# Splitting the column DFT of an FNet and gated-MLP kernel by the parity of its rows

## Chip, cores and metric

The kernel runs on one core of a Trainium2 chip, in one launch. The metric is device time in microseconds (us), the median of several runs. The engines are named as in the profile: PE is TensorE's matmul, PEld its weight load, DVE is VectorE, ACT is ScalarE, POOL is GpSimd, SP is SyncE, whose queue issues most of the DMA transfers.

## The reference

Four residual sublayers act on x of 2048 rows and 640 columns; the same two alternate twice.

```python
def mix(x):      # sublayer A: real part of a 2D DFT
    a = x @ hid_re.T ; b = x @ hid_im.T          # DFT over the 640 columns
    return seq_re @ a - seq_im @ b               # DFT over the 2048 rows, real part
def glu(x):      # sublayer B
    return (sigmoid(x @ w_gate) * (x @ w_up)) @ w_down     # 640 -> 1728 -> 640
x = x + mix(layernorm(x)); x = x + glu(layernorm(x))
x = x + mix(layernorm(x)); x = x + glu(layernorm(x))
```

The layernorms have no weights; eps is 1e-5. Everything is float32.

## The kernel before

x stays in SBUF as 16 tiles of 128 rows (`X`), in four row sets i of four groups A, B, C, D. A group holds rows that the symmetries of the row DFT pair with the others' rows, so one row set needs 128 rows of the DFT matrix. Each float32 operand of a matmul is split into two float16 parts, HI and LO, and each product is three matmuls (HI HI, HI LO, LO HI; `PASSES`). ACT makes the HI part and DVE the LO part (lines 241 and 243).

**A layer's mixing** has these steps. *Folding* normalizes a row set and adds or subtracts mirrored columns (`fold_columns`: e holds c and 640 - c added, o subtracted, 320 columns each; column 0 is doubled and appended to e) and mirrored rows (`fold_rows`, `fold_join`), and splits the result. *Sequence* (line 846) is the row DFT: for a row set i and a half tp (EV or OD, the even and odd output rows) it adds into three PSUM banks, one for each block d of 128 folded columns; row sets 0 and 1 make the sums ph = 0, row sets 2 and 3 ph = 1. *Eviction* (`evict_sums`) splits the sums into tiles z. *Hidden* (q, ph) is the column DFT (`product`, line 923): for r = 0 (real) and r = 1 (imaginary) it multiplies 128 rows of z with the folded column matrix, 321 output columns, over three blocks d of the contraction; 17 matmuls in all, since the last block of r = 1 has 64 rows and holds two parts in one tile. q 0 and 1 need the EV half, q 2 and 3 the OD half. `hidden_middle` does one row more. The products of ph = 0 and 1 are evicted separately; `combine` makes the difference and the sum of r = 0 and 1, `join_hidden` the sum or difference over ph, and `add_hidden` adds the 321 columns and their mirror images to x.

**The gated MLP** works in four blocks b of 512 rows. Block 0 begins with ordinary products (`gate_up`, line 1134); the first three tiles j are done in halves of 256 rows, since rows 0 and 1 are ready first. Later ones multiply 2 x 2 blocks in seven products instead of eight (line 1181). Then come the down products (line 1338), which add to x.

**The order** of the opening (loading and mixing of layer 0, to the first gate halves) is written out by hand as one list, `OPENING`: all instructions of all engines are issued in that order, and each engine works its own in order. In it `turn` are PE's row reversals, `col`, `double`, `re`, `ro`, `de`, `do`, `join`, `jhi`, `jlo` fold, `seq` is a sequence, `evhi` and `ev` evict sums, `hid` is a hidden product, `nst`, `npow`, `nscale`, `nrm`, `nhi`, `nlo` normalize, `tp` transposes, `gu` is a gate half, `wld`, `wshi`, `wslo` load and split a weight. After it `steps` lists PE's work in order, and `at(u, f)` puts another engine's job in front of step u. The layer change is the stretch between the last down product of layer 0 and the first gate half of layer 1; there `he` counts the steps.

**Space** in SBUF is one tile, `big`, in units of 128 float32 columns. Some places are fixed; the others come from `Slots`, which hands out space while the program is built: of the first few places that fit, it takes the one that was freed longest ago.

At the end the kernel tests that the given DFT matrices have the symmetries that it uses, and otherwise runs a general version.

Of the kernel before, what the change touches and what calls it, by code (L numbers as in the profile page):

```python
# [30 lines left out]
EC = EH + 1  # L31
EPS = 1e-5
# [39 lines left out]
FIX = XU + 2 * XTU + WDU  # L72


class Slots:

    LOOK = {4: 2, 5: 6}

    def __init__(self, big):
        self.big = big
        self.live = {}
        self.freed = {}
        self.clock = 0
        self.close = False

    def take(self, n, high):
        taken = sorted(self.live.values())
        if self.close:  # L90

            ends = [FIX] + [d for _, d in taken]
            free = [(a, b) for a, b in zip(ends, [c for c, _ in taken] + [UNITS]) if a + n <= b]
            assert free, f"no room for {n}: {taken}"
            if high:
                a = [a for a in range(UNITS - n, FIX - 1, -n) if all(a + n <= c or d <= a for c, d in taken)][:high]
                if a:
                    return self.new(min(a, key=lambda a: max(self.freed.get(u, 0) for u in range(a, a + n))), n)
                a = max(b for _, b in free) - n
            else:  # L100
                a = min((a for f in free for a in {f[0], f[1] - n}),
                        key=lambda a: (max(self.freed.get(u, 0) for u in range(a, a + n)), a))
            return self.new(a, n)
        found = []
        for i in range(UNITS):
            a = UNITS - (i + 1) * n if high else FIX + i * n
            if a < FIX or a + n > UNITS:
                break
            if all(a + n <= c or d <= a for c, d in taken):
                found.append(a)  # L110
                if len(found) == self.LOOK.get(n, 3):
                    break
        if not found:
            found = [a for a in range(FIX, UNITS - n + 1) if all(a + n <= c or d <= a for c, d in taken)][:1]
        assert found, f"no room for {n}: {taken}"
        age = lambda a: max(self.freed.get(u, 0) for u in range(a, a + n))
        return self.new(min(found, key=age), n)

    def new(self, a, n):
        s = Slot(self.big[:, a * UNIT : (a + n) * UNIT], (a, a + n))  # L120
        self.live[id(s)] = s.span
        return s

    def give(self, s):
        self.clock += 1
        del self.live[id(s)]
        for u in range(*s.span):
            self.freed[u] = self.clock


class Slot:
    def __init__(self, ap, span):
        self.f32, self.span = ap, span
        self.f16 = ap.bitcast(F16)
        n = self.f16.shape[1] // 2
        self.parts = (self.f16[:, :n], self.f16[:, n:])
# [16 lines left out]
    turn 0 B, turned 0 B, turn 0 C, turned 0 C, turn 1 B, chi 0 0, means 0, chi 1 0, square 0 C, stats 0 A,  # L153
    col 0 0, stats 0 D, turned 1 B, turn 1 C, col 0 1, clo 0 0, square 0 B, turned 1 C, clo 1 0, double 0 0,
    smeans 0, double 0 1, stats 1 A, means 1, stats 1 D, col 1 0, col 1 1, chi 1 1, square 1 B, clo 1 1,
    square 1 C, power 0, turn 2 B, double 1 1, turned 2 B, turn 2 C, scale 0, stats 2 A, ro 0 0, chi 1 2, chi 0 1,
    smeans 1, turned 2 C, whhi 1, col 2 0, double 1 0, power 1, re 0 0, clo 1 2, ro 0 1, scale 1, whhi 2, ro 1 1,
    col 2 1, re 1 0, re 1 1, ro 1 0, do 1 1, re 0 1, do 0 0, de 1 0, means 2, de 1 1, stats 2 D, square 2 B,
    do 1 0, de 0 1, de 0 0, join 1 o, square 2 C, whhi 5, do 0 1, join 0 e, row 0, join 0 o, smeans 2, whhi 0,
    join 1 e, whlo 1, whlo 0, row 1, double 2 0, power 2, jhi 0 e, jhi 0 o, turn 3 B, turned 3 B, c512hi, jhi 1 e,  # L160
    clo 0 1, turn 3 C, double 2 1, jhi 1 o, jlo 0 o, jlo 0 e, scale 2, col 3 0, row 2, jlo 1 o, turned 3 C, ro 2 1,
    re 2 1, jlo 1 e, col 3 1, chi 0 2, ro 2 0, re 2 0, whlo 5, de 2 1, do 2 0, double 3 0, seq 0 1, means 3,
    stats 3 A, do 2 1, double 3 1, seq 1 1, de 2 0, square 3 B, evhi 0 1 0, seq 0 0, join 2 o, join 2 e,
    square 3 C, wshi 0 1, stats 3 D, clo 0 2, row 3, whhi 3, whlo 2, ev 0 1 0, smeans 3, evhi 0 1 1, evhi 0 1 2,
    c512lo, ev 0 1 1, chi 1 3, whhi 4, jhi 2 o, whlo 3, whlo 4, ev 0 1 2, jhi 2 e, power 3, seq 1 0, wshi 2 0,
    scale 3, wshi 2 1, re 3 1, jlo 2 o, jlo 2 e, ro 3 1, chi 0 3, de 3 1, hid 3 0, evhi 0 0 0, evhi 0 0 2, do 3 1,
    re 3 0, clo 0 3, seq 2 1, ro 3 0, hidev 3 0, ev 0 0 0, clo 1 3, do 3 0, ev 0 0 2, join 3 o, de 3 0, evhi 0 0 1,
    jhi 3 o, ev 0 0 1, join 3 e, jhi 3 e, jlo 3 o, seq 2 0, wshi 1 0, jlo 3 e, hid 0 0, wslo 1 0, seq 3 0, difhi 0,
    wshi 1 1, evhi 1 0 0, evhi 1 0 1, wslo 1 1, dif 0, seq 3 1, evhi 1 0 2, ev 1 0 0, ev 1 0 1, ev 1 0 2,
    evhi 1 1 2, wslo 0 1, ev 1 1 2, evhi 1 1 0, evhi 1 1 1, hid 0 1, hid 1 0, ev 1 1 0, wld 3 1, difhi 1, ev 1 1 1,  # L170
    dif 1, sum 0, hid 2 0, wshi 0 0, add 0, hidev 1 0, hid 1 1, nst 0, sum 1, nst 1, npow 0, hidev 2 0, hidev 1 1,
    hid 3 1, add 1, nscale 0, hid 2 1, nrm 0, nst 3, nhi 0, nrm 1, wld 4 0, nhi 1, nst 2, nlo 0, nlo 1, tp 0,
    wslo 0 0, npow 1, wld 4 1, hidev 3 1, wshi 4 0, tpl 0, tp 1, midhi, tpl 1, nscale 1, tph 0, tph 1, wshi 4 1,
    hidev 2 1, nrm 2, mid, nhi 2, nrm 3, nhi 3, gu 0 0, middif, nlo 2, tp 2, wld 3 0, wslo 2 0, tpl 2, nlo 3,
    gu 1 0, tp 3, wshi 3 1, wshi 3 0, wslo 2 1, tph 2, tph 3, gu 2 0, wslo 3 1, tpl 3, gu 0 1, gu 1 1, gu 2 1,
    wslo 3 0, wslo 4 0, wslo 4 1"""

ON_ACT = {(2, GA), (2, GD), (3, GA), (3, GD)}
NORM_ACT, APPLY_ACT, COPY_ACT = {0, 3}, {3}, {3}
# [3 lines left out]
def kernel(ctx: ExitStack, tc: tile.TileContext, x, ct, wh, wg, wu, wc, wd, out):  # L183
# [7 lines left out]
    flag = pool.tile([P, 1], I32, name="flag")  # L191
    with tc.manual_schedule():
        folded(ctx, tc, pool, dram, big, acc, flag, x, ct, wh, wg, wu, wc, wd, out)
# [7 lines left out]
def folded(ctx, tc, pool, dram, big, acc, flag, x, ct, wh, wg, wu, wc, wd, out):  # L201
    nc = tc.nc
    slots = Slots(big)
# [3 lines left out]
    hs = pool.tile([P, 1], F32, name="hs")  # L207
# [77 lines left out]
    def drop(*key):  # L285
        s = held.pop(key if len(key) > 1 else key[0])
        if s.span:
            slots.give(s)
# [9 lines left out]
    def free_bank(*ks):  # L298
        banks.extend(ks)
# [297 lines left out]

    def folds(i):
        if (FE, i) not in held:
            if folding[0] and i < NB - 1:  # L600

                at = XU + i % 2 * XTU
                fixed(at, 11, FE, i)
# [1312 lines left out]
```

## Time and profile before

| what | value |
|---|---|
| time before, median of 3 runs | 1143.38 us (1143.14 to 1143.42) |
| span of the profiled execution | 1142.6 us, 23152 instructions |
| time outside the profiled span | the runs are 0.5 to 0.8 us over the span; the page gives no other time of that execution |
| mean granted clock of TensorE | 0.997 |
| matmuls of the column DFT (L923), 321 columns | 224 of 128 rows, 48 of 65 rows, 12 and 6 for the middle |
| matmuls of the row DFT (L846) | 288 |
| matmuls of the gates and down products (L1181, L1338, L1134) | 4698, 2624, 705 |
| DMA | 215.94 MB, 189 GB/s |

The profile gives busy time by engine, 40 slices of the span, and for groups of instructions the line, the operation, its shape, count, busy time and mean duration. [...] In an answer of the timeline a row is a run of like instructions on one engine: start, length, engine, line, operation, tiles, shape, count, and in brackets the idle time before it and what ended that. In the list of waits a row is: who waited, for whom, the total in us, how often, the longest.

### The profile page before, as it was taken

The numbers are of one execution on the slowest core, as the hardware profiler recorded it, in microseconds if no ns is written. First come the engines' busy times: TensorE is split into PE (matmuls) and PEld (weight loads), VectorE is DVE, ScalarE is ACT, GpSimd is POOL, SyncE is SP. The second block draws the span as 40 slices with busy tenths as digits, with TensorE's granted clock in tenths as the row PEclk, the third lists the DMA queues.
The fourth block names the chain that finished last, engine by engine and source line by source line (L and its number), as shares of the span: only waits on it lengthen the run. The fifth ranks groups of instructions, "written<-read, shape, count | busy, mean of one in ns | idle before, by whom it ended". The sixth has DMA issues, their size and how long they took to land.

```text
span 1142.6 us, 23152 instructions
## 1 busy us (share of the span) xinstructions
PE 1107.9 (97%) x8918; PEld 876.1 (77%) x8918; DVE 757.1 (66%) x1686; ACT 521.8 (46%) x1129; POOL 372.3 (33%) x584
## 2 busy tenths in 40 slices
PE   5599999999999999999999999999999999999997
PEld 2377446788878887888877888778887888788875
DVE  7995888867756777576657767815773568526740
ACT  5975475254524653265524445314551455225420
POOL 2313574432545454422430136021453113221000
PEclk9999999999999999999999999999999999999999
DMA  8427587858495868867412377575658853896401
GB/s 256 145 67 258 199 310 210 256 189 265 153 261 179 263 205 163 276 227 263 155 70 93 106 224 213 133 240 182 210 150 234 285 179 124 159 250 205 149 18 38
DMA packets 156434, 215.94 MB, mean 189 GB/s; under 512 B 74720, under 2 KB 101493, under 8 KB 156314
## 3 DMA queue, kind: packets, MB, share of 16 engines
q1 hardware_dynamic: 137754, 166.44, 48.1%
q0 software_dynamic: 18560, 47.93, 13.8%
q8 instruction: 72, 1.18, 0.4%
q14 instruction: 48, 0.39, 0.1%
HBM read 173.45 MB, written 26.26 MB: 175 GB/s over the span
## 4 chain that ended last, share of the span: by engine, by line
PE 89%; DVE 5%; DMA 2%; ACT 2%; issue 1%; POOL 1%; SPq 0%; DVEq 0%; POOLq 0%; ACTq 0%
PE acc L1181 42%; PE acc L1338 31%; PE acc L1134 10%; PE acc L1274 2%; PE acc L923 2%; PE acc L846 1%; DMA big<-in_ct 1%; DVE big L243 1%; PE twin L355 1%; DMA big<-kept_w 0%; DMA big<-in_wd 0%; DVE big L715 0%; DVE big L673 0%; DVE big L1009 0%; DVE big L707 0%
## 5 line engine op out<-in xcount | busy, mean ns | idle before, releaser
L1181 PE MATMUL acc<-big 128*128 128x256 f16 x4698 | 516.4, 273 | 0.2 <-ACT big L1185 0.2
L1181 PEld LDWEIGHTS <-big 128*128 128x128 f16 x4698 | 459.7, 98 | 54.6 <-issue 0.3
L1338 PE MATMUL acc<-big 128*128 128x320 f16 x2624 | 357.7, 299 | 0.0
L1338 PEld LDWEIGHTS <-big 128*128 128x128 f16 x2624 | 256.8, 98 | 99.5
L1387 POOL DMA_DIRECT2D big<-in_ct x256 | 174.8, 688 | 217.0 <-DVE big L1396 132.8
L1185 ACT ACTIVATE big<-acc 128x256 f32<-128x256 f32 x348 | 128.6, 380 | 237.0 <-PE acc L1181 235.6
L1371 ACT ACTIVATE big<-big 128x768 f32<-128x768 f32 (+8 forms) x104 | 79.6, 765 | 118.4 <-DVE big L1396 83.4
L1249 DVE TENSOR_TENSOR big<-big 128x512 f16<-128x512 f32 x87 | 59.9, 688 | 100.3 <-ACT big L1248 100.0
L1134 PE MATMUL acc<-big 128*128 128x256 f16 (+1 forms) x705 | 114.8, 325 | 1.1 <-DVE big L243 1.1
L1134 PEld LDWEIGHTS <-big 128*128 128x128 f16 x705 | 68.6, 98 | 46.2 <-DVE big L243 1.6
L1353 DVE SCALAR_TENSOR_TENSOR big<-acc,big 128x320 f32<-128x320 f32 x64 | 28.4, 484 | 99.4 <-PE acc L1338 99.3
L1227 ACT ACTIVATE big<-big 128x512 f32<-128x512 f32 x87 | 53.5, 627 | 45.2 <-DVE big L1218 44.6
L243 DVE SCALAR_TENSOR_TENSOR big<-big 128x640 f16<-128x640 f32 (+5 forms) x80 | 64.3, 839 | 9.9 <-ACT big L241 6.8
L241 ACT ACTIVATE big<-big 128x640 f16<-128x640 f32 (+6 forms) x80 | 50.2, 667 | 36.3 <-DMA big<-big 11.0
L1237 DVE SCALAR_TENSOR_TENSOR big<-acc,big 128x256 f32<-128x256 f32 x87 | 36.3, 418 | 40.5 <-PE acc L1181 34.4
L1404 POOL DMA_DIRECT2D big<-in_ct x40 | 27.3, 685 | 109.7 <-ACT big L1185 65.3
L1218 DVE TENSOR_TENSOR big<-big,acc 128x512 f32<-128x512 f32 x87 | 59.1, 679 | 3.6 <-PE acc L1181 3.4
L1248 ACT ACTIVATE big<-big 128x512 f16<-128x512 f32 x87 | 54.5, 626 | 9.6 <-DVE big L1239 8.8
L1217 DVE TENSOR_TENSOR big<-big 128x256 f32<-128x256 f32 x87 | 36.3, 417 | 15.6 <-ACT big L1185 15.5
L521 ACT ACTIVATE big<-big 128x384 f16<-128x384 f32 (+2 forms) x48 | 28.8, 648 | 29.3 <-DVE big L503 15.7
L1394 DVE TENSOR_TENSOR big<-big 128x256 f32<-128x256 f32 x64 | 26.8, 419 | 21.3 <-DMA big<-in_ct 21.2
L923 PE MATMUL acc<-big 128*128 128x321 f16 (+2 forms) x290 | 40.9, 300 | 0.0
(206 smaller groups left out, 1040.9 us busy)
## 6 DMA issues: line engine op xcount, KB each, us to landing
big<-kept_s SPq DMA_DIRECT2D x84, 512.0 KB
big<-kept_w SPq DMA_DIRECT2D x115, 320.0 KB
big<-in_ct POOLq DMA_DIRECT2D x256, 128.0 KB, 4.1
big<-kept_w SPq DMA_DIRECT2D x74, 192.0 KB
kept_w<-big SPq DMA_DIRECT2D x27, 320.0 KB
big<-in_ct POOLq DMA_DIRECT2D x32, 256.0 KB, 5.0
kept_s<-big SPq DMA_DIRECT2D x13, 512.0 KB
big<-in_wg SPq DMA_DIRECT2D x18, 320.0 KB
```

The lines of the kernel that those rows point to most:

```text
L243: nc.vector.scalar_tensor_tensor(dl, src, s, dh, op0=OP.mult, op1=OP.subtract)
L923: nc.tensor.matmul(ps[:m, :EC], z[:, at : at + m], w[:, 384 * wp : 384 * wp + EC], start=(d == 0 and zp == HI and wp == HI), stop=(d == ND ...
L1134: nc.tensor.matmul(ps, w[wp][:, d * P : (d + 1) * P], xt[:, xp, :], start=(d == 0 and wp == HI and xp == HI), stop=(d == ND - 1 and wp == LO))
L1181: nc.tensor.matmul(ps, wt, xt, start=start and n == 0, stop=n == len(todo) - 1, skip_group_check=not start)
L1185: nc.scalar.activation(dst, ps, AF.Copy)
L1218: nc.vector.tensor_tensor(v, v, other, op=OP.add)
L1227: nc.scalar.activation(v, v, AF.Sigmoid, scale=SG)
L1248: nc.scalar.activation(s.parts[HI], v, AF.Copy)
L1249: nc.vector.tensor_tensor(s.parts[LO], v, s.parts[HI], op=OP.subtract)
L1338: nc.tensor.matmul(held["pd", e][0][:, :EH], held["ht", j].parts[hp][:, i * P : (i + 1) * P], held["w", 2, j].parts[wp][:, e * EH : (e + 1 ...
L1371: nc.scalar.activation(v, v, AF.Square, accum_out=new_sum()[:p])
L1387: nc.gpsimd.dma_start(v[:, g], bass.AP(ct.tensor, (r * S + row) * S, [[P, NS], [d * S, 16], [1, P]]))
```

## The change

1. The 320 or 321 rows of the folded column matrix are sorted by parity. Output column 320 - k of an even row equals column k, and of an odd row it is column k negated. So even rows and odd rows are multiplied apart, for columns 0 to 160 only (161 columns, `EW`). Block d = 0 holds even rows, block 2 odd rows (161 columns each), block 1 both (322 columns, `EQ`; the rows of the wrong parity have scale 0). `unfold` makes the 321 columns by an addition and a subtraction. `fold_columns` writes the folded columns sorted by parity, reading every second column.
2. In the opening for all q, and in layer 1 for q = 0, the products of ph = 0 and 1 add into the same PSUM banks. After ph = 0 ACT copies the partial product; after ph = 1 the total is evicted, and the difference over ph comes as twice the part less the total.
3. The layer change begins with hidden (1, 0) and the odd half of row sets 0 and 1, which before stood ahead of the last down products; row set 3 is folded and joined for the even half first, and the last down product of layer 0 is done in two halves of columns. Hidden (0, 0) and (0, 1) follow, then the odd half; rows 0 and 1 are normalized first, rows 2 and 3 later. Hidden (3, 1) stands behind the first gate half.
4. `OPENING` has a new order. PE's order at its end, before and after:

```text
before: seq 0 1, 1 1, 0 0, 1 0, hid 3 0, seq 2 1, 2 0, hid 0 0, seq 3 0, 3 1, hid 0 1, 1 0, 2 0, 1 1, 3 1, 2 1,
        tp 0, tp 1, mid, gu 0 0, tp 2, gu 1 0, tp 3, gu 2 0, gu 0 1, gu 1 1, gu 2 1
after:  seq 0 1, 0 0, 1 1, 1 0, 2 1, 2 0, 3 0, 3 1, hid 0 0, 0 1, 1 0, 2 0, 1 1, 2 1,
        tp 0, tp 1, mid, gu 0 0, tp 2, gu 1 0, tp 3, hid 3 0, 3 1, gu 2 0, gu 0 1, gu 1 1, gu 2 1
```

5. The space of all tiles is planned ahead: the program is built once to record when each tile is taken and given back (counted in such events), `find_homes` gives each a place, and the program is built again with these places. In the first blocks of layer 1, the jobs that add row sets 2 and 3 to x come earlier.
6. The test at the end also covers the new symmetry (three more tests for each of r = 0 and 1).

The diff, cut to its core:

```diff
+EW = EH // 2 + 1
+EQ = 2 * EW
+NEAR = (60, 25, 8, 1)
...
+def find_homes(asked):
+    area = [n * (t1 - t0) for n, t0, t1 in asked]
+    for near in NEAR:
+        first = {}
+        for turn in range(40):
+            order = sorted(range(len(asked)), key=lambda k: (-first.get(k, 0), -area[k]))
+            homes, k = place_in_order(asked, order, near)
+            if k is None:
+                return homes
+            first[k] = first.get(k, 0) + 1
+def place_in_order(asked, order, near):
...
+            gap = min([t0 - u1 if u1 <= t0 else u0 - t1 for c, d, u0, u1 in placed if c < a + n and a < d] or [near])
+            rank = (min(gap, near), -a)
+            if best is None or rank > best[0]:
+                best = rank, a
...
     def product(ps, ph, r, at, m, more=False):
-        for d, n in enumerate(KT[r]):
+        for d, c in ((1, slice(0, EQ)), (0, slice(0, EW)), (2, slice(EW, EQ))):
+            n = KT[r][d]
...
-                    nc.tensor.matmul(ps[:m, :EC], z[:, at : at + m], w[:, 384 * wp : 384 * wp + EC],
+                    nc.tensor.matmul(ps[:m, c], z[:, at : at + m], w[:, 384 * wp : 384 * wp + c.stop - c.start],
...
     def hidden(q, ph):
         def mm():
-            pair = held["py", q, ph] = bank_pair()
-            for r in range(2):
-                product(pair[r][0], ph, r, sums_at(q, ph, r), P)
+            more = joined(q) and ph == 1
+            if not more:
+                held["py", q, ph] = bank_pair()
+            pair = held["py", q, 0 if more else ph]
+            for r in (1, 0) if q == 0 else (0, 1):
+                product(pair[r][0], ph, r, sums_at(q, ph, r), P, more)
...
+    def unfold(s, v, on=nc.vector):
+        on.tensor_tensor(s[:, :, :EW], v[:, :, :EW], v[:, :, EW:], op=OP.add)
+        on.tensor_tensor(s[:, ::-1, EH : EW - 1 : -1], v[:, :, : EW - 1], v[:, :, EW : EQ - 1], op=OP.subtract)
...
+    def first_sums():
+        (a, ka), (_, kb) = held.pop(("py", 0, 0))
+        o, t = pair_of(take(6, "sum", 0)), held["im"].f32[:, :EQ]
+        for n, op in enumerate((OP.subtract, OP.add)):
+            nc.vector.scalar_tensor_tensor(o[:, n], a[:, :EQ], CY, t, op0=OP.mult, op1=op)
...
     def join_hidden(q, cd):
         u, v = (pair_of(held["dif", q, ph]) for ph in range(2))
-        o = pair_of(take(6, "sum", q, cd))
-        nc.vector.tensor_tensor(o, u, v, op=OP.subtract if cd else OP.add)
+        if cd == 0 and q not in joins:
+            nc.vector.tensor_tensor(v, u, v, op=OP.add)
         if cd:
+            nc.vector.scalar_tensor_tensor(v, u, 2.0, v, op0=OP.mult, op1=OP.subtract)
...
+        unfold(whole_of(take(6, "out", q, cd)), v)
...
-            order = [(hidden, 0, 0), (hidden, 1, 0), (sequence, 2, EV), (sequence, 2, OD), (sequence, 3, EV),
-                     (sequence, 3, OD), (hidden, 0, 1), (hidden, 2, 0), (hidden, 3, 0), (hidden, 1, 1), (hidden, 2, 1),
-                     (hidden, 3, 1), (hidden_middle,)]
+            order = [(hidden, 1, 0), (sequence, 0, OD), (sequence, 1, OD), (sequence, 2, EV), (sequence, 3, EV),
+                     (hidden, 0, 0), (hidden, 0, 1), (sequence, 2, OD), (sequence, 3, OD), (hidden, 1, 1), (hidden, 2, 0),
+                     (hidden, 3, 0), (hidden_middle,), (hidden, 2, 1)]
             steps += [f(*a) for f, *a in order]
-            steps += [gate_up(0, j, (0,)) for j in range(3)]
+            steps += [gate_up(0, 0, (0,)), hidden(3, 1)] + [gate_up(0, j, (0,)) for j in (1, 2)]
...
-                steps += [sequence(*s) for s in early_sums]
+                steps += [sequence(i, EV) for i in range(2)]
...
-                at(block[0] + 1.6 + 0.8 * n if q == 1 else (block[0] + 14.6 if q == 2 else block[1] + 3.5) + n, f, q, *a)
+                at(block[0] + 1.6 + 0.8 * n if q == 1 else block[0] + (9.6 if q == 2 else 15.6) + n, f, q, *a)
```

422 lines of the change are left out of this document (256 added, 166 removed).

## Prediction

> **What bounds the kernel now.** I read the page's busy times and its slices first, then what TensorE (PE) waited for, then busy time by stretch, and last the timeline of PE.
>
> ```profile
> PE 1107.9 (97%) x8918; PEld 876.1 (77%) x8918; DVE 757.1 (66%) x1686; ACT 521.8 (46%) x1129; POOL 372.3 (33%) x584
> PE   5599999999999999999999999999999999999997
> ...
> PE acc L1181 <- ACT big L1185: 0.2, 1, 0.2
> ```
>
> PE is busy for 1107.9 us of a span of 1142.6. In the slices its idle time lies in the first two and the last; between them it waited 0.2 us for all the seven-product steps (L1181). So PE time saved in the middle would be time saved, unless something else comes due late. The change touches two places only: the opening and the layer change.
>
> ```profile
> 60.00:70.00 10.00, 9.50 (x84) 7.68 (x82) 9.97 (x19) 6.35 (x12) 0.00 (x0) 1.00 0.17 55
> 70.00:80.00 10.00, 10.00 (x76) 7.21 (x74) 9.68 (x17) 6.31 (x15) 1.24 (x2) 1.00 0.29 98
> ```
>
> The columns are stretch, length, busy time (and count) of PE, PEld, DVE, ACT and POOL, clock, DMA share and rate. From 60 to 70 us VectorE (DVE) is full and PE is not: the opening's front is DVE's. From 70 to 80 both are full, and neither can grow unseen.
>
> **The column products.** Seventeen matmuls of 321 columns become six of 322 and eleven of 161, in each of 16 products. The two middle products go from nine of 321 to three of 322 and six of 161.
>
> ```profile
> 603.73 4.82 PE L923 MATMUL acc<-big 128*128 128x321 f16 x34
> 608.38 4.89 PE L846 MATMUL acc<-big 128*128 128x256 f16 x41
> 613.56 3.56 PE L846 MATMUL acc<-big 128*128 128x256 f16 x31 [0.29 <-DVE big L715]
> 616.96 14.13 PE L923 MATMUL acc<-big 128*128 128x321 f16 x102
> ...
> 632.83 1.39 PE L923 MATMUL acc<-big 128*1 128x321 f16 x9
> 634.16 6.72 PE L1134 MATMUL acc<-big 128*128 128x256 f16 x60
> 640.72 1.40 PE L569 MATMUL acc<-ident,big 128*128 128x128 f16 x20
> ...
> L923 PE MATMUL acc<-big 128*128 128x321 f16 x224 | 34.1, 300 | 0.0
> ...
> L569 PE MATMUL acc<-ident,big 128*128 128x128 f16 x80 | 6.0, 220 | 0.4 <-DVE big L465 0.4
> ```
>
> A run's length less one matmul's own duration, over the others, is the spacing. 321 columns: (4.82 - 0.30)/33 = 137 ns. 128: (1.40 - 0.22)/19 = 62 ns. 256, from 60 in 6.72 us: 110 ns. No row has 161 columns; the line from 128 to 321 gives 62 + 33 x 0.39 = 75 ns, and half of 137 is 69. I take 72. A product goes from 17 x 137 = 2.33 us to 6 x 137 + 11 x 72 = 1.61, so 0.72 saved; a middle from 1.23 to 0.84. In all 16 x 0.72 + 2 x 0.39 = 12.3 us of PE, where PE sets the time.
>
> [...]
>
> **The layer change.** VectorE takes up the last down product at 603.79 (L1353, below) and the first gate half starts at 634.16: 30.4 us. In it PE did eight products (4.82 + 14.13 us), 72 sequence matmuls, 20 transposes, the middle, and waited some tenths (0.29 at 613.56). After the change, 36 matmuls of early sums come into this stretch, and it starts 36 x 0.11 = 4.0 us sooner. PE's work is 8 x 1.61 + 108 x 0.11 + 1.3 + 0.84 = 26.9 us. Without waits the gate half comes 30.4 - (26.9 - 4.0) = 7.5 us sooner. Two chains could take that back.
>
> The first runs from the last down product to row set 3's even half. It took 9.8 us (603.79 to 613.56).
>
> ```profile
> 603.79 0.89 DVE L1353 SCALAR_TENSOR_TENSOR big<-acc,big 128x320 f32<-128x320 f32 x2 [9.21 <-PE acc L1338]
> 604.60 0.87 DVE L420 BATCH_NORM_STATS2 quad<-big 128x6 f32<-128x320 f32 x2
> 605.51 0.21 DVE L421 BATCH_NORM_AGGREGATE quad<-quad 128x2 f32<-128x12 f32 x1
> ...
> 605.83 0.82 DVE L627 TENSOR_TENSOR big<-big 128x640 f32<-128x640 f32 x1
> ...
> 608.43 0.88 DVE L964 SCALAR_TENSOR_TENSOR big<-acc,big 128x321 f32<-128x321 f32 x2
> 610.18 1.69 DVE L707 TENSOR_TENSOR big<-big 128x321 f32<-128x321 f32 x4
> 611.88 1.62 DVE L715 TENSOR_TENSOR big<-big 128x642 f16<-128x642 f32 x2
> ```
>
> Half of the residual, of the statistics and of the two column folds now comes before the end, and half of the joins and splits after the even half: 0.44 + 0.44 + 0.82 + 0.84 + 0.81, and the 0.88 of L964 is gone. That leaves 5.6 us; with ACT's copies between, up to 7. The cover is one product and three sequences, 1.6 + 54 x 0.11 = 7.5 us, so it costs nothing; if the chain came out as before, it would cost 2.3.
>
> The second runs from the end of product 0 over both halves to the transposes of rows 0 and 1.
>
> ```profile
> 619.48 0.44 ACT L959 ACTIVATE big<-acc 128x321 f32<-128x321 f32 x1 [1.73 <-PE acc L923]
> ...
> 621.74 1.56 DVE L1009 TENSOR_TENSOR big<-big 128x642 f32<-128x642 f32 x2
> ...
> 623.34 0.74 ACT L430 ACTIVATE big<-big 128x640 f32<-128x640 f32 x1 [3.42 <-DVE big L1009]
> ...
> 624.20 0.83 ACT L431 ACTIVATE big<-big,small 128x640 f32<-128x640 f32 x1
> ...
> 625.74 0.72 POOL L404 TENSOR_TENSOR small<-small,half 128x2 f32<-128x2 f32 x1 [0.29 <-DVE small L403]
> 626.49 0.16 DVE L408 TENSOR_TENSOR small<-small 128x2 f32<-128x2 f32 x1 [0.84 <-POOL small L404]
> ...
> 63.42 0.68 DVE L243 SCALAR_TENSOR_TENSOR big<-acc,big 128x512 f16<-128x512 f32 x1
> ```
>
> Step by step: copy 0.44, sum and difference 0.89, two unfolds 0.88 (two halves of L707's kind), addition 1.56, row 1's statistics on ACT 1.8 (both passes with their read-outs), two small steps and the power 1.1, four small steps 0.8 (0.2 apart), one scaled copy 0.74, two low parts 1.6: 9.8 us. Three evictions of the odd half (0.68 each) stand in DVE's queue between: 11.4 with part of them hidden. PE's cover is two sequences and three products, 3.9 + 4.8 = 8.7, and 0.6 of transposes that run inside the wait. I take a wait of 2.0; it lies between none and 4. The gain here is 7.5 - 2.0 = 5.5 us, from 3.5 to 7.5.
>
> The new wait, product 0's second half behind ACT's copy of the first, is short: the products run r = 1 first, so a 0.44 copy has the 0.85 us of r = 0's nine matmuls to finish in. Queued behind it on PE are the sequences of the odd half, whose operands are ready by then. For rows 2 and 3 the same steps follow, with a doubling in place of the sums, again some 9.8 us; the cover is the middle, two products and two half-gates of 30 matmuls, 0.8 + 3.2 + 6.6 = 10.6. I book nothing, and 0.5 if it is short.
>
> **The opening.**
>
> ```profile
> 15.17 0.21 POOL L377 TENSOR_SCALAR quad<-quad 128x2 f32<-128x2 f32 x1 [3.38 <-ACT big L369]
> ...
> 34.48 2.88 POOL L377 TENSOR_SCALAR quad<-quad 128x4 f32<-128x4 f32 x1 [6.70 <-ACT big L369]
> ...
> 40.42 0.17 DVE L408 TENSOR_TENSOR quad<-quad 128x4 f32<-128x4 f32 x1 [0.18 <-POOL quad L404]
> ...
> 70.42 14.13 PE L923 MATMUL acc<-big 128*128 128x321 f16 x102
> ...
> 73.42 0.89 DVE L964 SCALAR_TENSOR_TENSOR big<-acc,big 128x321 f32<-128x321 f32 x2 [0.19 <-ACT big L959]
> ...
> 83.90 1.50 DVE L465 TENSOR_TENSOR big<-big 128x640 f16<-128x640 f32 x2
> ...
> 109.68 15.50 PE L1134 MATMUL acc<-big 128*128 128x512 f16 x71 [1.14 <-DVE big L243]
> ```
>
> Up to the last join the new list gives DVE the same work, less one eviction of 0.68. So the front ends 0.7 us sooner. The other end: a split (0.68) and two low parts (1.62 and a copy, 0.2) that stood before row set 2's scale (40.42, released by POOL) now stand after it; if POOL is no sooner, DVE is idle there for 2.5 us. I take the first: L377 took 0.21 us at 15.17 and 2.88 here, so POOL has that much to give back.
>
> The two products that PE did in the front's idle time (3 0, 0 0) now come later. After the sequences at 70.4 both products 0 follow, to 73.6, and the copy, 74.0. Then DVE: sums 0.89, unfolds 0.88, add 1.56, differences 0.88 and their doubling 0.8, statistics 1.09 (L420's two and L421), unfolds 0.88, add 1.56, an eviction 0.68, small steps 0.8, statistics 1.09, two low parts 1.64: 12.8, to 86.8, where L465 ended at 85.4. That is 1.4 later, 0.7 with the shorter front. PE's own four products end at 80, so it waits here for DVE, as it didn't before; product 2 1 also stands behind the eviction that DVE does after the second add. After the transposes PE has the middle's 0.4 us less and two products (3 0, 3 1) more, 3.2; the wait of 1.14 at 109.68 goes, since PE gets there later than its weights. Opening: 0.7 - 0.4 + 3.2 - 1.1 = 2.4 us lost, between -3.0 and +6.
>
> **What is hidden.** Folding and unfolding by two:
>
> ```profile
> 37.72 0.68 DVE L243 SCALAR_TENSOR_TENSOR big<-big 128x516 f16<-128x516 f32 x1
> ...
> 660.00:700.00 40.00, 40.00 (x361) 35.18 (x360) 25.94 (x63) 19.25 (x48) 15.69 (x23) 1.00 0.86 246
> ...
> SPq L1100 <- PE acc L1181: 111.8, 26, 15.0
> ...
> 262.50 5.51 DMA big<-kept_w
> ```
>
> L243's 516 elements are read every second one, and take the 0.68 us of the 512 read in a row: the strided folds cost nothing. In the second layer the unfolds add 1.76 us of DVE for each of three row sets (two of 0.88), 5.3 in all, in first blocks where DVE has 14 us idle in 40; at full DVE they would cost their 5.3. In the first layer it is half of that, as an addition goes for most of it. Six more checks of the column matrix stand beside the seven-product steps (the 0.2 us). The column matrix's loads carry half the bytes. In SP's queue two weight loads (3 1, 4 1) come to stand behind others that wait for splits of about the same time; if they came late, the 1.14 us at 109.68 would stay.
>
> Sum: 1143.4 - 5.5 + 2.4 = 1140.3 us, 3.1 less. The profiled span is 0.8 under the median of the runs; I carry the difference to the median. A measurement can tell 0.2%, 2.3 us: under 1141.1 is faster, over 1145.7 slower.
>
> **The rivals.** (1) Both chains fit under PE: 7.5 less at the layer change, and in the opening PE sets all after 70.4 (8 x 1.61 + 0.84 against 14.13 + 1.39, and no wait): 1.8 + 1.1 less. 1133.0. For: in the old chain DVE stood idle for POOL (0.84 at 626.49), and steps could fill that. Against: DVE's 9.68 of 10 us from 70 on.
>
> (2) Weight loads set the narrow matmuls:
>
> ```profile
> L923 PEld LDWEIGHTS <-big 128*128 128x128 f16 x224 | 21.9, 98 | 8.8 <-DVE big L243 0.2
> ```
>
> At 98 ns instead of 72, a product loses 0.29; eight at the layer change and four in the opening: 3.4 us, 1143.7, no change. For: 98 is what a load shows. Against: transposes at 62 ns with the same load.
>
> (3) The opening's front gets DVE's gap of 2.5 us and doesn't end 0.7 sooner: 3.2 more, 1143.5, no change. For: the scale waited for POOL before as well (0.18). Against: POOL's 0.21.
>
> (4) Slower: the planned homes. A load waits until the space that it gets is free, and all loads behind it on SP wait too. They wait now (111.8 us at L1100, 15.0 once), but PE feels 0.2. The chain passes through a load at 262.50 with no slack; a home freed only when the last reader before it is done would put its 5.51 us flight before PE, twice (weights and their sums) 11.0: 1151.3. It decides from 5.4 us on, one flight. For: the plan ranks by events, not by time. Against: it asks for up to 60 events between uses.
>
> **How the numbers follow.** Forecast 0.50, itself 1137.5 to 1142.5 (0.42 of it faster); (1) 0.11, (2) 0.08, (3) 0.12 (0.02 of it slower, where its tail adds), (4) 0.19. Faster 0.53, same 0.26, slower 0.21. The range leaves out (4) and the end of (1): 1134.0 to 1147.0.
>
> **What would show it.** Runs of product matmuls of 161 columns with about 72 ns spacing; PE busy for 12 us less; the first gate half 5 to 6 us nearer to the last down product's end, counted with the moved sums; PE idle before the transposes near 80 to 85 us; 512-column gates starting 2 us later than 109.68. It is wrong if PE waits for loads in the blocks, if the narrow matmuls space at 98, or if the opening's gates start earlier.

## The result: 1156.66 us, slower by 1.2%, and the profile after

| | before | after |
|---|---|---|
| median | 1143.39 us (1143.14 to 1143.42, 4 runs) | 1156.66 us (1155.6 to 1158.21, 4 runs) |
| profiled execution: span, own time | 1142.6 us, none shown | 1154.3 us, 1156.14 us |
| PE busy | 1107.9 us | 1101.6 us |

The ratio is 1.0116, interval 1.0101 to 1.013. The forecast was 1140.3 us, 1134.0 to 1147.0: wrong in sign. One remark on the sums: in later runs of the kernel before, 1.8 us lay between span and time (1142.0 and 1143.77, for one), so the profiled execution of before, at 1142.6, was probably some 1.0 us slower than the median, and a sum over the two profiles comes out nearer to 12 us than to the 13.3 of the medians.

First the page of the kernel after: busy time by engine, and PE's slices. The same rows of before stand in the prediction.

```profile
PE 1101.6 (95%) x8918; PEld 872.5 (76%) x8918; DVE 772.3 (67%) x1738; ACT 531.4 (46%) x1156; POOL 365.9 (32%) x573
PE   5479999999999999999999999999999999999997
```

PE is busy for 6.3 us less, and the span is 11.7 us longer: PE waits where it didn't. The list of its waits (total, how often, longest) has these among others; the first row is of before, at the same reversals of row sets. From 70 us on, before had one wait of 1.14 us at the first 512-column gates and some tenths elsewhere:

```profile
PE twin L355 <- ACT big L361: 12.0, 6, 7.5
```

```profile
PE twin L382 <- ACT big L388: 15.6, 6, 10.7
...
PE acc L1313 <- ACT big L1317: 4.2, 5, 1.2
...
PE acc L1266 <- ACT big L265: 2.9, 2, 2.5
...
PE acc L1003 <- DVE big L267: 2.1, 1, 2.1
PE acc L1003 <- ACT big L1054: 1.7, 1, 1.7
PE acc L1470 <- ACT big L1456: 1.6, 1, 1.6
```

L382 and L1003 are the opening, L1266 and L1470 layer 0's block 0, L1313 the seven-products, nearly all of it (3.6) in layer 1. Dividing the span at three places of PE's timeline gives a ledger in us (A: start to the first 512-column gate product; B: from there to the end of layer 0's down products; C: the layer change, to layer 1's first seven-product; D: the rest). In before, B holds 36 matmuls of early sums (4.0 us) that after has in C. The other columns are experiments told below; the last row has the medians. A to D are of one profiled execution each: the columns "mixed homes" and "+ three edits" have the same opening, and their A differs by 1.4 us.

| | before | after | mixed homes | + three edits | + front's order | + row set 3's product |
|---|---|---|---|---|---|---|
| A | 107.9 | 114.8 | 114.0 | 115.4 | 110.7 | 108.8 |
| B | 495.9 | 498.8 | 490.9 | 490.4 | 491.3 | 490.4 |
| C | 57.6 | 55.3 | 55.3 | 55.3 | 55.3 | 55.3 |
| D | 481.0 | 485.4 | 484.6 | 482.0 | 481.6 | 481.7 |
| median | 1143.4 | 1156.7 | 1147.4 | 1143.9 | 1140.1 | 1138.0 |

With the 4.0 us counted on the same side, after against before is +6.8 in A, +6.9 in B, -6.3 in C and +4.4 in D.

**C did what it should.** PE's timeline of after at the layer change:

```profile
613.38 1.76 PE L1003 MATMUL acc<-big 128*128 128x322 f16 x17
614.97 8.04 PE L921 MATMUL acc<-big 128*128 128x256 f16 x72
622.85 3.45 PE L1003 MATMUL acc<-big 128*128 128x322 f16 x34
...
634.84 0.44 PE L632 MATMUL acc<-ident,big 128*128 128x128 f16 x5
635.89 1.25 PE L632 MATMUL acc<-ident,big 128*128 128x128 f16 x15 [0.60 <-DVE big L510]
...
639.60 2.57 PE L1266 MATMUL acc<-big 128*128 128x256 f16 x22
```

A product takes 614.97 - 613.38 = 1.59 us, where 1.61 was forecast; neither chain keeps PE waiting for more than 0.6 us. The first gate half starts 26.1 us behind the last down product, where before took 30.3; with the 4.0 us of sums counted it is 8.2 us nearer, and 1.6 of these are product (3, 1), which now stands behind it.

### The profile page after: what moved, and what is told of

Same layout as the page of the kernel before. It is cut to its first block, busy times and chain, and to the rows that moved or that the text cites. A ratio compares the mean times of both kernels' runs of the same rounds, so it can differ in the third digit from the quotient of the medians.

```text
span 1154.3 us, 23256 instructions
## 1 busy us (share of the span) xinstructions
PE 1101.6 (95%) x8918; PEld 872.5 (76%) x8918; DVE 772.3 (67%) x1738; ACT 531.4 (46%) x1156; POOL 365.9 (32%) x573
## 5 line engine op out<-in xcount | busy, mean ns | idle before, releaser
L1313 PE MATMUL acc<-big 128*128 128x256 f16 x4698 | 516.8, 273 | 4.2 <-ACT big L1317 4.2
L1313 PEld LDWEIGHTS <-big 128*128 128x128 f16 x4698 | 459.6, 98 | 59.2 <-issue 5.1
L1470 PE MATMUL acc<-big 128*128 128x320 f16 x2624 | 357.9, 299 | 1.6 <-ACT big L1456 1.6
L1470 PEld LDWEIGHTS <-big 128*128 128x128 f16 x2624 | 256.7, 98 | 101.3 <-ACT big L1456 1.9
L1503 ACT ACTIVATE big<-big 128x768 f32<-128x768 f32 (+10 forms) x110 | 81.6, 742 | 120.3 <-DVE big L1528 86.8
L1266 PE MATMUL acc<-big 128*128 128x256 f16 (+1 forms) x705 | 117.0, 327 | 3.8 <-ACT big L265 2.9
L1266 PEld LDWEIGHTS <-big 128*128 128x128 f16 x705 | 68.5, 98 | 50.6 <-ACT big L265 3.9
L267 DVE SCALAR_TENSOR_TENSOR big<-big 128x640 f16<-128x640 f32 (+5 forms) x78 | 60.2, 801 | 15.7 <-ACT big L265 15.6
L265 ACT ACTIVATE big<-big 128x640 f16<-128x640 f32 (+7 forms) x78 | 48.9, 668 | 31.8 <-DMA kept_s<-big 12.1
L1369 DVE SCALAR_TENSOR_TENSOR big<-acc,big 128x256 f32<-128x256 f32 x87 | 36.3, 418 | 40.0 <-PE acc L1313 33.7
L1525 DVE TENSOR_TENSOR big<-big 128x256 f32<-128x256 f32 x64 | 26.6, 416 | 27.1 <-DMA big<-in_ct 21.5
L921 PE MATMUL acc<-big 128*128 128x256 f16 (+2 forms) x288 | 37.4, 290 | 7.4 <-ACT big L783 5.1
L1526 DVE TENSOR_TENSOR big<-big 128x256 f32<-128x256 f32 x64 | 26.8, 419 | 23.9 <-DMA big<-in_ct 23.8
```

The source lines that it names most:

```text
L265: nc.scalar.activation(dh, src, AF.Copy, scale=s)
L267: nc.vector.scalar_tensor_tensor(dl, src, s, dh, op0=OP.mult, op1=OP.subtract)
L1266: nc.tensor.matmul(ps, w[wp][:, d * P : (d + 1) * P], xt[:, xp, :], start=(d == 0 and wp == HI and xp == HI), stop=(d == ND - 1 and wp == LO))
L1313: nc.tensor.matmul(ps, wt, xt, start=start and n == 0, stop=n == len(todo) - 1, skip_group_check=not start)
L1470: nc.tensor.matmul(held["pd", e][0][:, :EH], held["ht", j].parts[hp][:, i * P : (i + 1) * P], held["w", 2, j].parts[wp][:, e * EH : (e + 1 ...
L1503: nc.scalar.activation(v, v, AF.Square, accum_out=new_sum()[:p])
```

## The experiments

**1. The homes.** Theory A put the loss in B down to the planned homes. Two kernels: the changed one with the homes after the opening chosen by the old kind of rule (of the first few places that fit, the one freed longest ago), and the kernel before with planned homes and nothing else.

```diff
-    return find_homes(asked)
+    return later_homes(asked, highs, find_homes(asked), since, CLOSED)
...
+        if asked[k][1] > since:
+            homes[k] = one_home(n, highs[k], sorted(live.values()), freed, when > closed)
```

> The changed kernel; only the places of tiles taken after the opening differ: they come from the rule of the kernel before (of the first few that fit, the one that has been free longest), the opening's stay as planned. From the first 512-column gate to the last down product of layer 0 the two kernels took 490.1 us (moved sums counted) and 498.6; from the first seven-product step of layer 1 to the end 480.9 and 485.5. Theory A, the planned places make loads in SyncE's queue wait for space, and what stands behind them: the first stretch falls to 490 to 492, the second to 481 to 483, the time to 1143.5 to 1147. Theory B, the added work on VectorE (unfolds, earlier additions) or the later opening makes the blocks slow: both stretches stay, 1155 to 1158.

Measured: 1147.4 us (1145.87 to 1148.2), ratio 1.0034 (1.0022 to 1.0046) to before. B falls by 7.9 us, all PE waits in it but one of 0.36 are gone; D falls by 0.8 only.

> The kernel before; only the places of all tiles are planned as in the changed kernel. Theory A: it loses in the blocks, 4 to 13 us, 1147 to 1156, with PE idle in front of L1134, L1181 or L1338. Theory B: 1143 to 1144.5.

Measured: 1155.65 us, ratio 1.0114 (1.0081 to 1.0147), with 505.8 in B, 9.9 more than before, and 483.0 in D. The plan alone makes the kernel before as slow as the changed one. So theory A stands for stretch B. For stretch D it had expected 481 to 483 us; the mixed-homes kernel takes 484.6 there, and experiment 3 takes that up.

**2. The end of the opening.** PE waits in it for ACT's copy and for an eviction; theory C said that issuing them sooner, and row set 3's products in the hole, would gain.

```diff
-    ... hid 2 0, evhi 1 1 2, ..., hid 1 1, nst 0, hidev 1 1, hidev 2 0, difs, ..., add 1, ev 1 1 2, ..., hid 2 1, ..., tp 3, ..., hid 3 0, hidev 3 0, hid 3 1, ...
+    ... evhi 1 1 2, ev 1 1 1, ev 1 1 0, ev 1 1 2, sums, out 0, hid 2 0, ..., hid 1 1, hidev 2 0, add 0, hid 2 1, ..., hid 3 0, ..., hid 3 1, ..., tp 0, ...
```

> The changed kernel with another order at the end of the opening: the copies of products 1 0 and 2 0 and the eviction ev 1 1 2 come before the first addition's statistics, the statistics of rows 0 and 1 before the differences, and products 3 0 and 3 1 stand before the transposes instead of behind tp 3. The places are planned anew by the same rule. Theory C, PE waited from 80 to 85 us for copies queued behind statistics and ran the 7 us after it at half the clock: no such wait, no stretch at half clock from 83.7 to 90.5, and the 512-column gates start at 109 to 111 instead of 114.9; the time 1150 to 1153 if the blocks stay as they are. Theory D, VectorE's total of work sets the opening: the transposes stay at 86 to 87 and the gates at 113 to 115, 1155 to 1158.

> Both edits together (opening filled as in the run before, places after the opening by the old rule). Theories A and C: about 1143.4 - 6.5 (layer change) + 0 (opening) + 1 (rest of the blocks, and time outside the span) = 1138 to 1141, faster than the kernel before. B or D: 1148 to 1155.

Measured: 1155.94 us (ratio 1.0109, 1.0091 to 1.0127) and, with the mixed homes, 1147.17 (1.0034, 1.0021 to 1.0047): no gain in either. The first transposes came at 88.48 instead of 86.70 us; the first 512-column gates at 114.53 and 114.73, against 114.78 and 113.98. The new order brings the transposes later (theory D had expected 86 to 87) and the gates no sooner: what was put ahead delays VectorE's and ScalarE's chain by as much as PE saves. Theory C falls: PE's order there isn't the cause.

**3. What was "hidden".** In the mixed-homes kernel, D has one wait in the list:

```profile
PE acc L1365 <- ACT big L1369: 3.0, 3, 1.3
```

Two of its places in the timeline (L1555 is the square of a test, L1369 the copy that PE waits for, L1580 and L1658 VectorE's part of tests, L1365 the seven-products):

```profile
710.89 0.84 ACT L1555 ACTIVATE big<-big 128x768 f32<-128x768 f32 x1 [3.80 <-DVE big L1580]
711.64 0.19 ACT L1555 ACTIVATION_READ_ACCUMULATOR big<-big 128x1 f32 x1
711.73 0.36 ACT L1369 ACTIVATE big<-acc 128x256 f32<-128x256 f32 x1
...
712.15 2.13 PE L1365 MATMUL acc<-big 128*128 128x256 f16 x18 [1.30 <-ACT big L1369]
...
1085.64 0.47 ACT L1555 ACTIVATE big<-big 1x319 f32<-1x319 f32 x1 [0.82 <-DVE big L1658]
...
1086.11 0.36 ACT L1369 ACTIVATE big<-acc 128x256 f32<-128x256 f32 x1
1086.52 2.45 PE L1365 MATMUL acc<-big 128*128 128x256 f16 x21 [1.14 <-ACT big L1369]
```

A test's square waits for VectorE, and the copy stands behind it in ScalarE's queue. By the rows around these, VectorE is late near 711 through the additions that the change moved here, and near 1086 through the new parity test.

```diff
-        square_sum(b)
+        rest.append(b)
...
-                at(... block[0] + (9.6 if q == 2 else 15.6) + n, f, q, *a)
+                at(... (block[0] + 14.6 if q == 2 else block[1] + 3.5) + n, f, q, *a)
...
-    homes = homes_for((x, ct, wh, wg, wu, wc, wd, out))
+    homes = HOMES
```

> Three edits to the mixed-homes version (1147.4 us, its second layer from the first seven-product to the end 484.6 us), each in a place of its own. (1) The additions of row sets 2 and 3 at the times of before, (2) the new parity test's first square moved from ScalarE's queue into the list of squares done later, (3) the homes written as a list of numbers, so that the program is traced once. Theory F: the second layer lost 3.0 us in three waits of TensorE for a ScalarE copy (the longest 1.3 us near 711 us, 1.14 us near 1086 us) that stands in ScalarE's in-order queue behind a test's square, which waits for VectorE; with the additions later and the square aside the three waits go and the second layer takes 481 to 482 us. Theory G: the second layer is longer because more VectorE work is in it (282.9 us busy against 273.2), wherever it stands; then it stays at 484 to 485. For the list: if tracing the program twice causes the time outside the span (1.8 us in the four kernels that trace twice, 0.8 in the kernel before), it falls to 0.8; if the difference has another cause in the changed code it stays at 1.8. Sum by F and the list: 1143.4 us; by G and no effect of the list: 1147.4.

Measured: 1143.92 us (1142.91 to 1145.9), ratio 1.0007 (0.9997 to 1.0016). D is 482.0, and two waits of together 0.9 us are left: F stands. The additions and the square were moved in one kernel, so the share of each isn't known. The list of numbers did nothing: time and span are 1.8 us apart still, as they are in the kernel before, so there was nothing to explain.

**4. The opening's front.** The kernel of experiment 3 with the order of the kernel before up to the last sequence matmuls; in the first kernel row set 3 is not joined over both halves, so that its even product can stand in the front as before; in the second its odd product stands ahead of the transposes as well; in the third row set 3 stays joined, and the order alone is changed. This order has product 0 0 back ahead of row set 3's sequences too, where before had it. The homes are planned anew for each order, by the same rule. The order, cut to two places, and the edit of the first two kernels:

```diff
-    ... turn 1 B, means 0, col 0 0, col 0 1, chi 1 0, square 0 C, stats 0 A, stats 0 D, ...
+    ... turn 1 B, chi 0 0, means 0, chi 1 0, square 0 C, stats 0 A, col 0 0, stats 0 D, turned 1 B, turn 1 C, col 0 1, clo 0 0, ...
...
-    ... seq 3 0, ..., seq 3 1, ..., wslo 0 1, hid 0 0, ...
+    ... jlo 3 e, hid 0 0, wslo 1 0, seq 3 0, ..., seq 3 1, ...
...
-        return q == 0 or not folding[0]
+        return q == 0 or (q < 3 and not folding[0])
```

> The version with the three edits, and in addition the opening's order up to the last sequence matmuls taken from the kernel before, which needs row set 3's even product in its old place in the front: row set 3 alone doesn't accumulate over both halves there. Theory H: the front's loss is the order alone. The last sequence matmuls end at 70.6 us instead of 71.1 to 72.1, TensorE has one product (1.6 us) less to do behind the transposes, and the first 512-column gate product begins near 111 us instead of 114: 2 to 3 us off the total. Theory I: VectorE's and ScalarE's chain behind the last sequence matmuls sets that time, whatever TensorE has done before; then the first transposes still come 14.5 us behind the last sequence matmuls, and only the 0.5 to 1.5 us of the front is won, the total falling by at most 1.5 us.

> The same, with row set 3's odd product also put ahead of the transposes, where TensorE waits for VectorE's low halves of rows 0 and 1. Theory H: the product costs nothing there (the stretch had 3.9 us of idle time), so the first 512-column gate product begins 1.5 us earlier than in the version without it, near 109.5 us. Theory I: its eviction comes into ScalarE's queue ahead of the copies that the gate products wait for, and the win is 0 to 0.5 us.

> The version with the three edits aside, with the kernel before's order of the front, but row set 3 joined over both halves as in the changed kernel, so that both its products stay behind the transposes. If the order alone made the front late (H), the last sequence matmuls end at 70.6 to 71 us, TensorE idles in the front for the product's 1.6 us more than in the version with it, and the first 512-column gate product begins 1.5 to 2 us later than the 108.8 us there: 110.3 to 111, total 1139.5 to 1140.5. If the product in the front mattered more than its own length (rival J: without it TensorE's clock or the chain falls back), it begins near 113 to 115 us and the total is 1142 to 1144.

Measured: 1137.97 us (ratio 0.9958, 0.9944 to 0.9971), 1137.91 (0.9958, 0.9945 to 0.9972) and 1140.12 (0.9972, 0.9962 to 0.9982). The first 512-column gates start at 108.8, 107.4 and 110.7 us. The third kernel came out as H said (110.3 to 111), which rules out J: the order alone is worth 3.8 us (1143.92 - 1140.12), row set 3's product in the front 2.2 more. Together they gave 6.0, twice what H expected of the first kernel. The odd product ahead of the transposes brings 1.4 in its profile, no more than two profiles of one opening differ by, and nothing in the medians, as theory I said. All three are faster than before and after.

Why the order matters is in VectorE's list of waits over the first 42 us, of before, after and the order alone; each row is VectorE's column fold waiting for ScalarE's copies of the reversed columns:

```profile
DVE big L627 <- ACT big L361: 2.6, 3, 1.5
```

```profile
DVE big L698 <- ACT big L388: 5.8, 3, 2.4
```

```profile
DVE big L775 <- ACT big L465: 2.5, 3, 1.4
```

The lists give VectorE the same work, but before puts statistics and a low part between the first folds, and after puts the folds first, where they wait. VectorE loses 3.3 us there against the order alone, and the last sequence matmuls (row set 3) end 3.7 us later, at 72.08 against 68.37. The clock doesn't make the difference: from 45 to 72 us the mean granted clock is 0.87 in both. Their rows, of after and of the order alone:

```profile
68.19 3.89 PE L921 MATMUL acc<-big 128*128 128x256 f16 x34 [0.51 <-DVE big L789]
```

```profile
64.48 3.89 PE L998 MATMUL acc<-big 128*128 128x256 f16 x34 [0.56 <-DVE big L866]
```

The first transposes come 5.2 us sooner in the order alone. Beside the 3.7 us, 1.5 are left, about the 1.6 of product 0 0, which it does in the front. The rows of the transposes in before and after, then both in the order alone:

```profile
84.39 1.52 PE L569 MATMUL acc<-ident,big 128*128 128x128 f16 x20
```

```profile
86.70 0.71 PE L632 MATMUL acc<-ident,big 128*128 128x128 f16 x5
```

```profile
61.94 1.75 PE L1080 MATMUL acc<-big 128*128 128x322 f16 x17 [1.43 <-DVE big L344]
...
81.48 0.71 PE L709 MATMUL acc<-ident,big 128*128 128x128 f16 x5 [0.93 <-ACT big L584]
```

**5. How a home costs time.** In the kernel after a store of summed weights went out late behind a load. Is the store's place in SyncE's queue the cause, or the load? The store was put on GpSimd's queue, then on ScalarE's.

```diff
-        nc.sync.dma_start(kept[key], v)
+        (nc.gpsimd if key[0] == "s" else nc.sync).dma_start(kept[key], v)
```

> The changed kernel with one edit: the stores of the summed weights (kept_s) are issued on GpSimd's queue instead of SyncE's; the planned homes stay. Theory A: the first layer's loss (498.8 us from the first 512-column gate product to the end of the products down, against 490.9 with the later tiles' homes chosen by the old rule) comes from these stores standing in SyncE's in-order queue behind loads that wait for their planned home; then TensorE's waits near 169 to 201 us (2.45 us and five smaller ones) go, the stretch takes 490 to 493 us and the total is 1148 to 1151 us. Rival K: the loads themselves land too late, or the waits come from GpSimd's sums whose home is reused too soon; then the stretch stays at 497 to 500 us and the total at 1155 to 1158.

> The changed kernel with one edit: the stores of the summed weights (kept_s) are issued on ScalarE's queue instead of SyncE's; the planned homes stay. On GpSimd's queue the store still went out at 159.3 us, since there it stood behind the next tile's sums, so that run couldn't tell. The store's data are ready when VectorE's low half of the sums ends, near 157 us in the changed kernel. Theory A (the store behind the load on SyncE): the store goes out 2 us sooner, and ScalarE's wait of 10.5 us for it falls by as much; the stretch from the first 512-column gate product to the end of the products down falls from 498.8 to 494 to 497 us. Rival K (the load itself, held for 8.6 us until GpSimd's sums release its home, is what makes the weight's splits and all behind them late, and the store only follows): the stretch stays at 497.5 to 500 us.

On GpSimd: 1154.64 us (ratio 1.0101, 1.0086 to 1.0117), B 497.9; the store went out at 159.3 as before the edit, behind the next tile's sums, so this run told nothing. On ScalarE: 1159.91 us (1154.32 to 1160.7; ratio 1.0127, 1.0103 to 1.0152), B 500.8. Rows of the timeline, first of after (L1204 to L1207 are GpSimd's sums, L1161 and L1163 loads of weights, L283 stores, L265 splits), with the row of SyncE's waits behind it; then of the store on ScalarE; then of before:

```profile
150.45 5.38 POOL L1205 TENSOR_TENSOR big<-big 128x256 f32<-128x256 f32 x1
155.91 1.98 POOL L1206 TENSOR_TENSOR big<-big 128x256 f32<-128x256 f32 x1
157.92 0.33 SPq L1161 DMA_DIRECT2D big<-in_wg  x1
...
159.11 0.42 SPq L283 DMA_DIRECT2D kept_s<-big  x1
164.06 1.15 ACT L265 ACTIVATE big<-big 128x256 f16<-128x256 f32 x2 [10.54 <-DMA kept_s<-big]
169.20 1.04 PE L1266 MATMUL acc<-big 128*128 128x512 f16 x2 [2.45 <-ACT big L265]
```

```profile
SPq L1161 <- POOL big L1206: 8.6, 1, 8.6
```

```profile
150.69 0.33 ACTq L283 DMA_DIRECT2D kept_s<-big  x1
...
160.35 0.33 SPq L1161 DMA_DIRECT2D big<-in_wg  x1
...
161.16 0.84 ACT L265 ACTIVATE big<-big 128x768 f16<-128x768 f32 x1 [5.23 <-POOL big L1207]
...
167.02 0.63 ACT L1290 ACTIVATE big<-big 128x512 f16<-128x512 f32 x1 [5.02 <-DMA big<-in_wd]
...
171.11 0.60 PE L1266 MATMUL acc<-big 128*128 128x512 f16 x2 [2.27 <-ACT big L265]
```

```profile
141.04 0.45 SPq L1029 DMA_DIRECT2D big<-in_wg  x1
```

```profile
142.12 2.71 POOL L1072 TENSOR_TENSOR big<-big 128x256 f32<-128x256 f32 x1 [4.75 <-DVE big L243]
144.79 5.38 POOL L1073 TENSOR_TENSOR big<-big 128x256 f32<-128x256 f32 x1
```

With the store at 150.69 ScalarE's wait of 10.54 us for it is gone, and PE stalls all the same: the load still goes out at 160.35, when GpSimd's sums let go of its home, and what stands behind it on SyncE lands at 167. Theory A in its form with the store falls, and K is left. The load is the twelfth of a gate weight, that of tile j = 11. The sums were as slow before (5.38), but there the twelfth load had another home and went out at 141.04, ahead of them. The plan finds no room when it asks for 60 or 25 events between uses, and is made with 8, and 8 lie between the give-back of this home (by the up weight of tile j = 8) and the load (the gate weight of j = 11). Another home for this load alone wasn't tried, so K is argued from these rows and not shown by a run of its own.

**6. PE's clock.** While PE waited near 80 us its granted clock also fell to half (0.50 from 83.69 to 90.52 us in the kernel after, below). Here its two holes there are filled with 33 matmuls whose results are dropped.

```diff
-    ... hid 2 1, ...
+    ... fill 15, filled 18, hid 2 1, ...
```

> The version with the front of before (1137.97 us), and 33 matmuls of 128x256 that compute nothing of use (their result is dropped) in the two holes in front of the first transposes, where TensorE waits 1.79 us for a ScalarE copy and 2.07 us for a VectorE low half: 15 ahead of product 2 1, 18 in it ahead of its last low part; at 110 ns each they fill 1.65 and 2.0 us. In that version TensorE was busy for less than half of the stretch 76.3 to 79.7 us and ran at half clock from 79.7 to 86.6. Theory L: TensorE's part-time work causes the half clock, and the half clock costs time here: with the holes filled the clock stays at 1.0, the 9 matmuls of 65 rows take 1.0 us instead of 1.8, the 15 transposes about 1.1 instead of 1.8, the middle 1.0 instead of 1.8, and the first 512-column gate product begins 1.5 to 2.5 us sooner (106.3 to 107.3); total about 1136. Rival M: the VectorE and ScalarE chain sets that stretch, so the clock stays full but the gain is under 0.5 us; or the clock halves all the same.

Measured: 1138.69 us (ratio 0.9958, 0.9944 to 0.9972), the same as without. By the lengths of PE's runs the half clock near 80 us is gone, as L says (15 transposes in 1.25 us instead of 1.78, 9 matmuls of 65 rows in 1.01 instead of 1.79), and the total gains nothing, as M says: the transposes start 13.24 us behind the last sequence matmuls in both, and the first 512-column gates 0.7 us sooner, counted from the transposes.

## Why the prediction was wrong, step by step

Three terms that the sum put at nothing failed: the homes, the work called hidden, and the order of the opening's front. The terms that it worked out came nearer.

**The column products**: 1.59 us against 1.61. 98 ns to a narrow matmul (rival 2) would give 1.90, and is out. PE's saving in busy time is 6.3 instead of 12.3, and most of the rest went to half clock: apart from the last 15 us, PE was busy for 13.3 us in five windows at half clock in after and for 3.4 us in one in before, and half of the difference, 4.9 us, is an estimate of what that took (from the 9 matmuls that took 1.80 us at a clock of 0.50 and 1.01 with the holes filled, last section). In the kernel with the holes filled (experiment 6), whose mean clock is that of before (0.997), PE is busy for 1099.6 us, of which 33 x 0.11 = 3.6 fill: 11.9 less than before.

**The layer change**: -6.3 against -5.5. The wait taken at 2.0 was 0.6, the term that was too large; the first chain cost nothing, as booked.

**The opening** was booked at +2.4, of which -1.1 is the wait at 109.68 that falls into B; so +3.5 in A, and measured is +6.8. The step that failed is "Up to the last join the new list gives DVE the same work": the amount was the same, the order was not. I looked for the gap at row set 2's scale, where VectorE waited 0.16 us; it lies in the first 20 us, as 3.3 us of waits for ScalarE. The two products behind the transposes (3.35 us for 34 matmuls), the gone wait at 109.68 and the idle PE at 80 to 85 us came as told.

With the order of before in its place A is 110.7, +2.8 for a booking of 3.5, and that this is so near is luck. Its transposes come 2.9 us sooner than before's, where 0.7 later was booked (1.4 - 0.7); product 0 0, booked as later, is back in the front there. From the transposes to the first 512-column gates it takes 5.7 us more than before, where 2.8 were booked (3.2 - 0.4): by the lengths of its runs PE worked for some 6 us of it, from 81.48 us on, at half clock (15 transposes in 1.78 us, 1.25 with the holes filled; 30 matmuls of 256 columns in 4.37, 3.45 in before), which is an estimate of 3 us more. In after itself the two are +2.3 and +4.5.

**What is hidden**, booked at nothing, cost 3.5 us (1147.4 - 1143.9; the profiles show 2.6 of it in D). I compared VectorE's idle time with the added work. But PE's copy stands on ScalarE behind a square that stands behind VectorE: ScalarE's square waited 3.80 us for VectorE near 711 and 0.82 near 1086, and PE waited 1.30 and 1.14 us for the copy behind it.

**The homes**, rival 4, priced at 11.0 and given 0.19: they cost 9.3 us (1156.7 - 1147.4), 7.9 of it in layer 0. The rows of experiment 5 show a load held as the rival describes, for 8.6 us in block 0, and PE's first stall behind it; that this load makes all of it isn't shown. The argument against it, "up to 60 events between uses", was the demand and not what the plan got (8), which could have been worked out ahead from the list of tiles.

With the three undone, the kernel takes 1140.12 us; the forecast was 1140.3. The three costs, 9.3 + 3.5 + 3.8 us, add up to the 16.5 between 1156.66 and 1140.12 because they are steps of one chain of kernels, so their sum proves nothing further. That the end lies at the forecast is in part luck: the layer change came 0.8 us better than booked, and in the opening two misses of some 3 us cancel, one of them helped by product 0 0 back in the front.

## What to carry to other kernels

Work on an engine with spare time can still cost time, when something that the bounding engine needs stands behind it in an in-order queue on the way (here 2.6 us of D); follow the queue, not the busy share. When a hand-written order changes, compare what each in-order engine waits for in the first stretch, even where the list of work is the same (here VectorE waited 3.3 us more). A plan for memory that counts events has to be held against time: look at what the slowest engine still reads when the load that gets its place is due, and at what stands behind that load (here it was held for 8.6 us).

## What the runs showed of the hardware

In the kernel after PE's granted clock was 0.50 from 83.69 to 90.52 us and from 169.02 to 172.43, both times behind a stretch in which PE worked part of the time. Windows, cut where the clock changed and every 3.41 us between (columns as in the prediction's):

```profile
76.87:80.28 3.41, 3.18 (x34) 2.61 (x33) 3.34 (x6) 1.74 (x4) 0.00 (x0) 1.00 0.00 0
80.28:83.69 3.41, 0.92 (x8) 0.59 (x7) 3.31 (x8) 3.19 (x8) 1.46 (x3) 1.00 0.00 0
83.69:87.10 3.41, 2.20 (x14) 1.53 (x14) 3.02 (x10) 2.93 (x6) 0.67 (x3) 0.50 0.00 0
87.10:90.52 3.42, 3.21 (x25) 2.31 (x24) 3.41 (x6) 2.99 (x5) 3.36 (x4) 0.50 0.01 2
...
165.61:169.02 3.41, 1.13 (x6) 0.29 (x3) 3.41 (x4) 3.38 (x8) 2.43 (x3) 1.00 0.98 294
169.02:172.43 3.41, 2.91 (x7) 0.87 (x8) 2.50 (x4) 1.88 (x5) 1.49 (x2) 0.50 0.95 381
```

PE was busy for 0.92 and 1.13 us of a window of 3.41, and the next was at half clock; behind 2.20 us busy in the first window at half clock there was one more. PE's own work behind a wait took longer there as well: the 9 matmuls of 65 rows behind the wait of 2.07 us took 1.80 us in after, and 1.01 with the holes filled. In that stretch another engine's chain set the time, and the total gained nothing when the holes were filled (1138.69 us, 1137.97 without). The row of these 9 matmuls, of after and with the holes filled:

```profile
84.76 1.80 PE L1003 MATMUL acc<-big 65*128 65x161 f16 x9 [2.07 <-DVE big L267]
```

```profile
80.64 1.01 PE L1084 MATMUL acc<-big 65*128 65x161 f16 x9
```
